# Idle products of 512 columns, and single chunk slots in the blocks from column 768 on

## The chip, the core and the metric

The kernel runs on one core of a Trainium2 chip. The core has five engines with queues of their own: TensorE (PE, matrix products; its weight loads are listed apart as PEld), VectorE (DVE), ScalarE (ACT), GpSimd (POOL) and SyncE (SP), which here issues nearly all DMA transfers. Products land in PSUM, of which the kernel's pools hold eight banks; DVE and ACT carry results from there to SBUF. The metric is the time of one execution on the device in microseconds, smaller being better.

## The reference

Two layers in a row. The first is a retention layer: for batch 8, 8 heads, 576 positions and head width 64,

```
scores = (q @ k.T) / sqrt(64)
D[i, j] = gamma_h ** (i - j)  if i >= j  else 0,   gamma_h = 1 - 2 ** (-5 - h)
x = (scores * D) @ v                    # laid out as 4608 tokens x 512
```

The second is a gated feed-forward layer on these 4608 tokens, with 1536 hidden columns:

```
out = (sigmoid(x @ w_gate) * (x @ w_val)) @ w_out     # 4608 x 512
```

Inputs and output are float32; products are made in bfloat16 with float32 sums.

## The kernel before

The decay is split into a factor on q and one on k (`qtab`, `ktab`), so that POOL and DVE, which cast q, k and v to bfloat16, multiply it in. The retention layer then runs in chunks of positions with a running state: the chunk's own part is `scores` (L476, tile row, PE line 483), a triangular `mask` on DVE (L495, tile pt) and `intra` (L504, tile val, PE line 509); what earlier chunks give is `inter` (L514, PE line 525), which multiplies q by the kept state; `products` (L486, PE line 491) makes the chunk's addition to the state, which `add_state` adds on DVE and `keep_state` casts (tile sb). The result is laid down transposed in `xT`, 512 by 4608, as the feed-forward layer wants it.

The first 768 columns of `xT` come from pairs of 128 positions, written out by hand (L816 to L998). The other columns come from 30 steps (`STEPS`), each with two pieces of 64 positions; step s fills the columns from 768 + 128 s on (the last two swapped). In the last piece of a batch (step 6 is the first of these) there is no `products`.

The feed-forward layer goes through `xT` in blocks of columns (`BLOCKS`, L1000): 256 columns at 512, 384 at 768 and at 1152, then 512 each. Within a block, `h_units` (L683) makes the gate and value products for 12 groups of hidden columns, and `op_units` (L746) the output products, 12 for each 128 tokens. Each of them yields after a unit: in the blocks of 384, 24 units of four h products, then 9 units of four op products. They use three PSUM banks (`ffn`) in turn. After the value product DVE multiplies by the sigmoid that ACT made (tile gv, L726).

Between these units, the loop from L1005 on places the chunk work, and this is what sets the order on all engines; there is no planner, the program's order is each queue's order. Two forms exist:

- `next_slot(s)` (L665, `slot` L529): one step. `intra` and `inter` of step s-1, then `scores`, `products` and `mask` of step s. The copies that empty the banks (`after`, L615) are put into `pending`, three parts, one for each later unit at which something may be placed. From step 6 on, the state casts of `after` go to POOL, before that to ACT.
- `next_two(vals, news)` (L675, `slot_of_two` L543): the values of up to two steps and the scores of two new ones in one group, with its copies in `after_two`. It uses two more banks for the second new step.

The values of a step stand in two PSUM banks (`VALS`), of which there is one each; the scores in two more (`ROWS`). In units of h of the larger blocks only every second unit takes something. In the block at 512 the loop places slots 0 to 3 (`SINGLE = 4`); every later block places two groups of two among its op units: ([3],[4,5]) and ([4,5],[6,7]) at 768, ([6,7],[8,9]) and ([8,9],[10,11]) at 1152, and so on, where the first list has the steps whose values are made and the second the new ones.

`casts_to(s)` (L654) issues, up to step s, the loads (SP), the casts (POOL), the DMA transpose of q and k (SP, tile T) and the cast of v. It is called ahead of the step that needs them, and at the start of each block from 768 on.

At the very start nothing can be computed until q and k are loaded. There `fill(n)` (L179) puts idle products on PE, of a zero tile into a spare bank that nobody reads; `fill` stands also between the first transposes and score products (L832 to L850). In all 24 units of n are issued.

## Time and profile before

| what | value |
|---|---|
| median of four runs | 329.26 us (329.12 to 330.04) |
| profiled execution | 329.12 us, of which the profile's span is 327.4 us |
| PE busy | 317.8 us, 97% of the span |
| DVE, ACT, POOL busy | 147.3, 139.6, 103.1 us |
| idle products (L182) | 96, 8.8 us busy, in the first 13 us |
| h products of the blocks (L698) | 426 and 426 recorded, 100.3 us busy each |
| op products (L765) | 353 recorded, 80.6 us busy |
| DMA moved | 55.16 MB, 168 GB/s in the mean |

A line of the timeline has the start and the length in us, the engine, the line of the kernel, the operation, what it writes and reads, the shape of the array used, the columns and the count; in brackets stands the idle time of the engine before it and what ended it. Products are pipelined: the length of one (219 ns for 128 columns, 379 ns for 512, at full speed) is longer than the step to the next, which is what counts in a stream. A few records of products are missing, which shows in the counts.

### The profile page before, as it was taken

How to read it: one execution, taken by the hardware profiler on the slowest of the kernel's cores; microseconds unless marked ns; L12 is line 12 of the kernel's file. 1: busy time of each engine (PE TensorE's matmuls, PEld its weight loads, DVE VectorE, ACT ScalarE, POOL GpSimd, SP SyncE). 2: the span in 40 equal slices, each digit the busy share in tenths (PEclk: the TensorE clock that was granted, in tenths of full speed). 3: DMA queues.
4: the chain of work that ended last, by engine and by line, in shares of the span. 5: the costliest groups of instructions: out<-in, count | busy, mean ns of one | idle time of the engine just before them, and what ended most of it. 6: DMA issues, size and time to landing. Idle time of an engine off the chain costs nothing.

```text
span 327.4 us, 8864 instructions
## 1 busy us (share of the span) xinstructions
PE 317.8 (97%) x3660; PEld 173.6 (53%) x3696; DVE 147.3 (45%) x331; ACT 139.6 (43%) x308; POOL 103.1 (31%) x136
## 2 busy tenths in 40 slices
PE   8899999999999999999999999999999999999995
PEld 8764457856655554455444544454445544544443
DVE  6845656654454463445334533444344433404410
ACT  6654545553344353324532553335334533343321
POOL 5674646453644093018200840074103000000000
PEclk9999999999999999999999999999999999999999
DMA  7999999999999689919791799169904910010003
GB/s 226 332 367 356 379 269 226 196 179 200 232 188 218 156 143 209 230 35 162 200 256 28 150 213 259 27 104 213 218 16 103 342 41 2 34 75 25 1 32 98
DMA packets 144794, 55.16 MB, mean 168 GB/s; under 512 B 125168, under 2 KB 136688, under 8 KB 144752
## 3 DMA queue, kind: packets, MB, share of 16 engines
q1 hardware_dynamic: 144608, 54.44, 69.9%
q8 instruction: 29, 0.48, 0.6%
q10 hardware_dynamic: 144, 0.13, 0.1%
q14 instruction: 13, 0.11, 0.1%
HBM read 37.75 MB, written 9.44 MB: 144 GB/s over the span
## 4 chain that ended last, share of the span: by engine, by line
PE 95%; ACT 1%; issue 1%; DVE 1%; ACTq 0%
PE h L698 50%; PE op L765 24%; PE op L952 3%; PE hv L802 3%; PE hg L802 3%; PE val L509 2%; PE idle L182 2%; PE row L483 1%; PE row L491 1%; PE val L525 1%; PE op L754 1%; PE qkp L329 1%; ACT qT L320 1%; PE hg L881 1%; PE hv L881 1%
## 5 line engine op out<-in xcount | busy, mean ns | idle before, releaser
L726 DVE TENSOR_TENSOR gv<-g,h 128x512 bf16<-128x512 bf16 (+1 forms) x96 | 62.8, 654 | 112.5 <-PE h L698 108.8
L698 PE MATMUL h<-xT,wg_sb 128*128 128x512 bf16 (+2 forms) x426 | 100.3, 355 | 0.3
L698 PE MATMUL h<-xT,wv_sb 128*128 128x512 bf16 (+2 forms) x426 | 100.3, 355 | 0.3
L722 ACT ACTIVATE g<-h 128x512 bf16<-128x512 f32 (+1 forms) x96 | 54.7, 570 | 93.6 <-PE h L698 83.1
L765 PE MATMUL op<-wo_sb,gv 128*128 128x512 bf16 x353 | 80.6, 379 | 2.5 <-issue 2.4
L698 PEld LDWEIGHTS <-wv_sb 128*128 128x128 bf16 x432 | 42.3, 98 | 40.7
L698 PEld LDWEIGHTS <-wg_sb 128*128 128x128 bf16 x432 | 42.0, 98 | 41.2
L765 PEld LDWEIGHTS <-gv 128*128 128x128 bf16 x372 | 35.2, 98 | 40.6
L288 POOL CAST v<-v 128x512 bf16<-128x512 f32 x29 | 17.7, 609 | 87.7 <-PE val L509 81.9
L283 POOL TENSOR_TENSOR qk<-k,ktab 128x512 bf16<-128x512 f32 x30 | 31.3, 1042 | 41.3 <-DMA k<-in_k_dram 28.6
L741 ACT COPY ob<-op 128x512 f32<-128x512 f32 x33 | 19.3, 585 | 32.9 <-PE op L765 30.0
L283 POOL TENSOR_TENSOR qk<-q,qtab 128x512 bf16<-128x512 f32 x28 | 29.2, 1042 | 2.5 <-DMA q<-in_q_dram 2.4
L567 ACT CAST xT<-val 128x256 bf16<-128x256 f32 x54 | 17.5, 381 | 26.7 <-PE val L525 19.8
L498 DVE TENSOR_TENSOR pt<-row,tri 128x256 bf16<-128x256 f32 x60 | 21.5, 418 | 2.4 <-PE row L491 1.5
L610 DVE TENSOR_TENSOR s<-s,row 128x256 f32<-128x256 f32 x39 | 16.3, 418 | 1.3
L459 ACT CAST sb<-s 128x256 bf16<-128x256 f32 x46 | 16.4, 421 | 0.2
L553 DVE COPY glance<-val 128x1 f32<-128x1 f32 x28 | 3.2, 154 | 26.5 <-PE val L525 23.6
L952 PE MATMUL op<-wo_sb,gv 128*128 128x512 bf16 x45 | 11.4, 379 | 0.3 <-issue 0.2
L525 PE MATMUL val<-T,sb 64*64 64x64 bf16 x368 | 10.0, 195 | 0.3 <-DVE glance L553 0.3
L509 PEld LDWEIGHTS <-v 64*64 64x64 bf16 x480 | 6.2, 108 | 7.1 <-issue 7.1
L809 DVE TENSOR_TENSOR gv<-g,hv 128x512 bf16<-128x512 bf16 x10 | 6.7, 684 | 7.0 <-PE hv L802 7.0
L182 PE MATMUL idle<-blank 128*128 128x128 bf16 x96 | 8.8, 262 | 1.1 <-DVE blank L170 1.1
(101 smaller groups left out, 235.1 us busy)
## 6 DMA issues: line engine op xcount, KB each, us to landing
out_dram<-ob SPq DMA_DIRECT2D x31, 256.0 KB, 3.6
k<-in_k_dram SPq DMA_DIRECT2D x26, 256.0 KB, 3.8
q<-in_q_dram SPq DMA_DIRECT2D x26, 256.0 KB, 4.0
v<-in_v_dram SPq DMA_DIRECT2D x26, 256.0 KB, 4.5
wg<-in_moe_w_gate_dram SPq DMA_DIRECT2D x12, 256.0 KB, 5.4
wv<-in_moe_w_val_dram SPq DMA_DIRECT2D x12, 256.0 KB, 5.1
wo<-in_moe_w_out_dram SPq DMA_DIRECT2D x12, 256.0 KB, 5.0
k32p<-in_k_dram SPq DMA_DIRECT2D x6, 256.0 KB, 5.0
```

Source lines behind the costliest of these rows:

```text
L283: eng.tensor_tensor(out=natural_qk[s][:, i].rearrange("p m (y d) -> p y m d", y=2), in0=by_halves(loaded[s][1 - i]), in1=tab, op=ALU.mult)
L288: eng(out=natural["v", s], in_=loaded[s][2])
L459: eng(out=state[key], in_=src)
L498: nc.vector.tensor_tensor(out=probs[s][:, y], in0=row_ps[s][y][:, 0], in1=tri.unsqueeze(1).to_broadcast([P, M, 64]), op=ALU.mult)
L567: nc.scalar.copy(out=xT[:, :, cols_of(s, i)], in_=val_ps[s][i])
L698: nc.tensor.matmul(out, lhsT=w_sb[:, kc, fc * P:(fc + 1) * P], rhs=xT[:, kc, t0 + a:t0 + e], start=(kc == 0), stop=(kc == NKC - 1))
L722: nc.scalar.activation(out=g[:, 0:n], in_=h1[:, 0:n], func=AF.Sigmoid)
L726: nc.vector.tensor_tensor(out=gvs[some[0]][:, a:e], in0=g[:, 0:n], in1=h2[:, 0:n], op=ALU.mult)
L741: (eng or on_act)(out=ob, in_=opp)
L765: nc.tensor.matmul(opp, lhsT=gvs[fc][:, nb * P:(nb + 1) * P], rhs=wo_sb[:, fc, :], start=(fc == 0), stop=(fc == NFC - 1))
L802: nc.tensor.matmul(ps, lhsT=(wg_sb if what == "g" else wv_sb)[:, kc, fc * P:(fc + 1) * P], rhs=xT[:, kc, 0:4 * P], start=(kc == 0), stop=( ...
L952: nc.tensor.matmul(opps[nb], lhsT=gvs[fc][:, nb * P:(nb + 1) * P], rhs=wo_sb[:, fc, :], start=(fc == 0), stop=(fc == NFC - 1))
```

## The change

It has two parts. First, a unit of `fill` is one product of 512 columns (the zero tile read four times over, into a whole bank), where it was four products of 128 columns. In all 24 products in place of 96.

Second, `SINGLE` becomes a list: the block at 512 places four single slots as before, the block at 768 three (4, 5, 6, at its h units 0, 10 and 20) and no group of two, the block at 1152 one (slot 7, at its h unit 0) and then the groups ([7],[8,9]) and ([8,9],[10,11]). From there on the groups are those of before. `casts_to` is no longer called at the start of a block; a group of two or a slot calls it alone. The spacing rule counts 5 units of 2048 from a block's end instead of 4, which leaves the slots of the block at 512 where they were.

```diff
     def idle_bank():
-        idle.append(ffn_psum.tile([P, P], FP32, tag="ffn", name=f"idle_{len(idle)}"))
+        idle.append(ffn_psum.tile([P, 4, P], FP32, tag="ffn", name=f"idle_{len(idle)}"))
...
     def fill(n):
 
-        for i in range(4 * n):
-            nc.tensor.matmul(idle[-1], lhsT=blank, rhs=blank, start=True, stop=True)
+        for i in range(n):
+            nc.tensor.matmul(idle[-1], lhsT=blank, rhs=blank.unsqueeze(1).to_broadcast([P, 4, P]), start=True, stop=True)
...
-    SINGLE = 4
+    SINGLE = [4, 3, 1]
...
-        end = slots + (SINGLE if w == 0 else 0)
+        end = slots + (SINGLE[w] if w < len(SINGLE) else 0)
...
-        if w == 0:
+        if w < 2:
             twos = []
-        else:
-            casts_to(slots + LEAD_CAST + 1)
...
-            elif slots < end and gone * (end - begin) >= (slots - begin) * (total - 4 * 2048):
+            elif slots < end and gone * (end - begin) >= (slots - begin) * (total - 5 * 2048):
                 next_slot(slots)
```

In the order of instructions on each engine, SP's queue is the same as before; POOL has two more instructions (the state casts of step 7, ahead of the casts of step 11), ACT ten more and DVE four more, since single slots copy their values in more and smaller pieces; PE has 72 products and 72 weight loads fewer, all idle ones.

## The prediction

> **What bounds the kernel now.** I read the shares of busy time first, then the chain of work that ended last, then TensorE's own timeline stretch by stretch. The first two say that TensorE (PE) is the limit nearly everywhere:

> ```profile
> PE 317.8 (97%) x3660; PEld 173.6 (53%) x3696; DVE 147.3 (45%) x331; ACT 139.6 (43%) x308; POOL 103.1 (31%) x136
> ...
> PE 95%; ACT 1%; issue 1%; DVE 1%; ACTq 0%
> ```

> So the price of an edit is what it does to PE's own queue, plus any wait that it makes PE meet. The change has two places: the idle products in the first 13 us, and the blocks from column 768 on. PE's timeline of the start (start, length, engine, line, tile, count):

> ```profile
> 1.05 4.45 PE L182 MATMUL idle<-blank 128*128 128x128 bf16 x40 [1.05 <-DVE blank L170]
> 5.29 0.63 PE L310 MATMUL kTp<-ident,kp 128*128 128x128 bf16 x4
> ...
> 6.14 1.03 PE L182 MATMUL idle<-blank 128*128 128x128 bf16 x12
> 7.25 0.42 PE L329 MATMUL qkp<-qT,kT 64*64 64x128 bf16 x16
> ...
> 7.83 0.61 PE L182 MATMUL idle<-blank 128*128 128x128 bf16 x8
> 8.28 0.39 PE L310 MATMUL qTp<-ident,qp 128*128 128x128 bf16 x4
> 8.50 0.83 PE L182 MATMUL idle<-blank 128*128 128x128 bf16 x12
> 9.49 0.42 PE L329 MATMUL qkp<-qT,kT 64*64 64x128 bf16 x16 [0.16 <-ACT qT L320]
> ...
> 12.36 0.83 PE L182 MATMUL idle<-blank 128*128 128x128 bf16 x12
> 13.12 0.41 PE L416 MATMUL pvp<-ptp,vp 64*64 64x128 bf16 x8
> ...
> 25.03 3.62 PE L802 MATMUL hg<-xT,wg_sb 128*128 128x512 bf16 x16
> ```

> The reader should see the step from one product to the next. The first 40 take 5.29 - 1.05 = 4.24 us, 106 ns each. The twelve from 8.50 last 0.83 us, of which the last one's own 0.219 us (the shortest of this group): 0.61/11 = 56 ns each. TensorE runs at half speed at first and at full speed from somewhere inside the twelve that begin at 6.14 (1.03 us is between the two rates). The last line gives products of 512 columns at full speed: 3.62 less 0.38 for the last, over 15, is 216 ns.

> The other place, from the same view further on:

> ```profile
> 58.24 0.60 PE L698 MATMUL h<-xT,wv_sb 128*128 128x256 bf16 x4
> 58.77 0.32 PE L509 MATMUL val<-pt,v 64*64 64x64 bf16 x16
> ...
> 59.43 0.61 PE L698 MATMUL h<-xT,wg_sb 128*128 128x256 bf16 x4
> ...
> 63.41 0.31 PE L509 MATMUL val<-pt,v 64*64 64x64 bf16 x14 [0.17 <-DVE xT L597]
> ...
> 71.75 0.81 PE L698 MATMUL h<-xT,wg_sb 128*128 128x384 bf16 x4
> 72.40 0.81 PE L698 MATMUL h<-xT,wv_sb 128*128 128x384 bf16 x4
> ```

> ```profile
> 93.77 0.32 PE L509 MATMUL val<-pt,v 64*64 64x64 bf16 x16
> ...
> 95.25 2.54 PE L765 MATMUL op<-wo_sb,gv 128*128 128x512 bf16 x11 [0.16 <-issue]
> 97.62 0.81 PE L698 MATMUL h<-xT,wg_sb 128*128 128x384 bf16 x4
> ...
> 123.69 1.03 PE L698 MATMUL h<-xT,wg_sb 128*128 128x512 bf16 x4
> ```

> Here the blocks begin at 71.75, 97.62 and 123.69, so they last 25.87 and 26.07 us. Their large products alone take 96 x 0.1625 (four in 0.65) + 36 x 0.216 = 23.38 us. What is left, 2.49 and 2.69 us, is two groups of chunk products each, and nothing else: PE never waits in these blocks. The "0.16 issue" before the line with x11 is a lost record (twelve were issued), not a wait.

> **The change, part by part.**

> *Idle products.* 72 products and 72 weight loads go; a unit of `fill` is one product of 512 columns, where it was four of 128. At half speed four steps are 0.427 us; a step of 512 at half speed is not in the trace, and twice its full-speed 0.216 is 0.432: no difference. At full speed a unit is 4 x 0.0558 = 0.223 against 0.216, 7 ns less. Most units hide something anyway: `fill(3)` at 6.14 and 8.50 and `fill(2)` at 10.30 end before ACT's qT or kT copy, which the next product waits for (9.49 line). On PE's path at full speed lie `fill(2)` at 7.83, `fill(1)` at 11.90, `fill(3)` at 12.36: six units, -0.04 us. The first `fill(10)` is also on the path: POOL's kp is ready at 3.77 + 1.04 = 4.81, and PE comes to it at 5.29; as long as before, it costs 0.

> [...]

> What the trace can't show is whether the other shape moves the moment of full speed. Bounds from rows: were it early enough for the first fill to end by 4.81, PE would gain 0.45 us there, but the next k tile is cast on POOL at 6.22 to 7.26 after its DMA, so the transposes at 7.59 could move to 7.30 at best: -0.3 us. Were it late, after 9.3, what PE does from 7.25 to 8.50 (1.25 us, all on the path) would take about twice as long: +1.2 less the 0.2 that waits for ACT, +1.0. The four runs of before spread over 0.92 us, which is about this. I take 0, since in either shape PE has no gap from 1.05 to 6.96.

> *Blocks.* Groups ([3],[4,5]) and ([4,5],[6,7]) of the block at 768, and ([6,7],[8,9]) of the next, become single slots 4, 5, 6 (units 0, 10, 20 of the block at 768), slot 7 (unit 0 of the next) and ([7],[8,9]). The products are the same 328. Price of before: the second group runs from 93.77, less 0.09 to enter, to 95.25 less the lost 0.216: 1.36. The first is 2.49 - 1.36 = 1.13. The group ([8,9],[10,11]) by the same reckoning (119.88 to 121.31) is 1.31, which leaves 1.38 for ([6,7],[8,9]). Sum 3.87.

> Price of after, from the single slots that stand before column 768. Slot 1, 64 products: PE could go on with h at 58.24 + 0.437 = 58.68 and does at 59.43: 0.75. Slot 0, 32 products: 52.95 + 0.437 to 53.86, 0.47. So about 9 ns a product and 0.19 for going in and out. Slots 4, 5 and 7 have 64 products, 0.75 each; slot 6, a last chunk without state products, 48: 0.61. Group ([7],[8,9]) has 88, eight fewer than ([3],[4,5]): 1.13 - 0.07 = 1.06. Sum 3.92, so +0.05. Bounds: the groups' internal delays vanish in ([7],[8,9]) (0.19 + 88 x 0.0088 = 0.96), -0.05; two groups more at 0.19 each and nothing else changed, +0.38. I take +0.05, by the row of a real slot.

> What is moved along with it. SP's queue keeps its order, DMA for DMA, so no load, transpose or store passes another. POOL gets two state casts of slot 7 ahead of the casts of chunk 11: they wait for DVE until about 101, and chunk 11, cast at 96.92 before, ends near 105; its transpose, at the longest landing (5.7 us) after an issue near 105, is there by 111, and PE wants it near 120. Chunk 4's transpose is issued from 64.26 and lands by 70.0; slot 4 wants it near 72.6. Chunks 5 and 6: issued at 71.42 and 76.98, wanted near 79.7 and 86.9. On ACT and DVE the copies of four slots now stand between sigmoids and gate products: in a pair of units (1.30 us of PE) ACT has 0.49 + 0.68 at most, DVE 0.56 + 0.28 + 0.41 = 1.25, and a bank of h is wanted again one pair later. The mask of a slot (0.75) falls into a pair that is itself 0.75 longer. All of it costs 0 while these margins hold.

> Sum: 329.12 (the profiled execution, span 327.4 and 1.7 around it) - 0.04 + 0.05 = 329.1. That execution is 0.14 below the median, so I expect a median of 329.2. About 0.2%, 0.66 us, is what a measurement of this kernel can tell from no change; 0.01 is far below it.

> **Rivals.**

> *Slots wait for a value bank (slower).* There is one bank each for the two halves of a chunk's values; slot s can't begin before the copies of slot s-1 have left them. Slot 2 shows the price: 62.49 + 0.437 = 62.93 to 64.06 is 1.13, 0.38 more than slot 1, and the releaser in the 63.41 line is DVE's leave_other. With four slots, +1.5: 330.7. Against it: slot 2 follows slot 1's last copy directly, where slot 4 has a unit of output products and one of h between (copies end at 70.96, slot at 72.4) and the others six units. It decides when DVE or ACT falls back by 1.4 us in slot 4, by 3.9 in the others.

> *Full speed comes later (slower).* Up to +1.0, 330.2; for it, only that the moment is not the program's to set; against it, PE is as full as before.

> *Full speed comes earlier (faster).* -0.3 at most by the DMA behind the second k tile: 328.9, still no change by the bound. To end on the faster side, the slots must also be cheaper than the groups by 0.4, or the idle stretches really shrink.

> *The moved groups buy nothing and cost the extra entries.* +0.38, 329.6: no change by the bound.

> **How the numbers follow.** Forecast as summed: 0.50. Early speed, 0.08, and the extra entries, 0.08, stay within 0.66 us too: 0.66 together. Slots that wait: 0.12. Late full speed in most runs: 0.08. Shorter idle stretches or cheaper slots, beyond 0.66: 0.14. So faster 0.14, same 0.66, slower 0.20. The range goes from 328.7 (early speed and the lower bound of the slots, with the spread of runs) to 330.2 (late speed, or two of four slots waiting).

> **What would show it.** Right: idle x10 from 1.05 to about 5.3 and a step of 216 ns later; h at 768 beginning near 71.7; slots near 72.5, 79.7, 86.9 and 98.1, each delaying h by 0.75; the blocks at 768 and 1152 lasting 23.38 + 2.11 = 25.5 and 23.38 + 0.75 + 1.06 + 1.31 = 26.5 us; no PE wait on DVE or ACT in them. Wrong: h at 768 beginning more than 0.5 us off 71.7 (the start moved), or a named wait ahead of val or h between 72 and 124 (the slots stall).

## The result and the profile after

The changed kernel takes 330.21 us in the median of 37 runs (329.13 to 333.22), the one before 329.25 us (59 runs, 328.64 to 330.36). The ratio is 1.0035, with a 95% interval of 1.0026 to 1.0045: slower by 0.35%, where I had forecast no change. (The ratio is not that of the two medians, which is 1.0029; it lies close to that of the means, so the long runs weigh in it.) The profiled execution took 329.93 us, its span 328.2 us, 0.8 us above that of before.

The runs of the changed kernel are of two kinds, told apart by the granted clock, the share of full speed that TensorE was given: of 38 with a record of the clock, 28 have a mean of 0.998 or more and a median of 329.87 us; ten have 0.993 to 0.995 and take 331.2 to 333.2 us. Of 74 runs of before that were made beside the experiments none has a clock below 0.998. So there are two amounts to explain: about 0.6 us in every run, and 2 us more in a quarter of them.

First the places that I had named. The page of the profile after, its busy times, two of its DMA queues and its chain:

```profile
span 328.2 us, 8732 instructions
...
PE 318.5 (97%) x3590; PEld 168.4 (51%) x3624; DVE 149.5 (46%) x335; ACT 139.1 (42%) x314; POOL 104.7 (32%) x138
...
q1 hardware_dynamic: 144608, 54.44, 69.6%
q8 instruction: 28, 0.46, 0.6%
...
PE 95%; issue 1%; ACT 1%; DVE 1%; ACTq 0%
```

TensorE is still the bound, with 0.7 us more of busy time. (ACT has 314 instructions where it had 308, six more and not ten.) The line to remember is that of queue 8, which moves instructions: 28 transfers, where the page of before has 29:

```profile
q8 instruction: 29, 0.48, 0.6%
```
The blocks, in TensorE's timeline after (start, length, engine, line, operation, tiles, array shape, columns, count):

```profile
72.47 0.81 PE L698 MATMUL h<-xT,wg_sb 128*128 128x384 bf16 x4
73.21 0.32 PE L509 MATMUL val<-pt,v 64*64 64x64 bf16 x16
...
73.89 0.82 PE L698 MATMUL h<-xT,wv_sb 128*128 128x384 bf16 x4
...
87.79 0.32 PE L509 MATMUL val<-pt,v 64*64 64x64 bf16 x16
...
98.03 0.81 PE L698 MATMUL h<-xT,wg_sb 128*128 128x384 bf16 x4
98.78 0.32 PE L509 MATMUL val<-pt,v 64*64 64x64 bf16 x16
...
99.46 0.82 PE L698 MATMUL h<-xT,wv_sb 128*128 128x384 bf16 x4
...
124.59 1.03 PE L698 MATMUL h<-xT,wg_sb 128*128 128x512 bf16 x4
```

The blocks last 98.03 - 72.47 = 25.56 and 124.59 - 98.03 = 26.56 us (forecast: 25.5 and 26.5). A slot of 64 products puts h off by 0.77 us (73.89 - 72.47 - 0.65), the shorter one at 87.79 by 0.60. No line of these blocks has a wait on DVE or ACT ahead of it. Together they take 52.12 us, where they took 51.94: +0.18.

The rest had happened before they began: h at 768 starts at 72.47, not 71.75, 0.72 us late. The start, in the same view:

```profile
1.05 4.45 PE L182 MATMUL idle<-blank 128*128 128x512 bf16 x10 [1.05 <-DVE blank L170]
5.29 0.63 PE L310 MATMUL kTp<-ident,kp 128*128 128x128 bf16 x4
...
7.23 0.42 PE L329 MATMUL qkp<-qT,kT 64*64 64x128 bf16 x16
...
15.13 0.44 PE L348 MATMUL st<-vp,kp 64*64 64x64 bf16 x16 [0.65 <-ACT sbd L358]
...
16.40 0.35 PE L348 MATMUL st<-vp,kp 64*64 64x64 bf16 x11
17.24 0.25 PE L348 MATMUL st<-vp,kp 64*64 64x64 bf16 x5 [0.49 <-issue]
17.43 0.40 PE L426 MATMUL pvp<-qT,sbd 128*128 128x128 bf16 x4
```

Up to the first score products everything is where it was (5.29 as before, 7.23 for 7.25). Then sixteen equal products, which write one tile and read two that were ready long ago, fall apart into eleven and five. The eleventh starts at 16.556, the twelfth at 17.240, where the step is 0.016 in the mean ((0.44 - 0.20)/15). "issue" says that the profile knows nothing that the engine waited for. In the timeline of before the same sixteen are one line:

```profile
16.22 0.44 PE L348 MATMUL st<-vp,kp 64*64 64x64 bf16 x16
16.59 0.40 PE L426 MATMUL pvp<-qT,sbd 128*128 128x128 bf16 x4
```

In the view of waits the second line here is the one entry of TensorE's in this stretch that before doesn't have (what waited, on what, us in total, times, longest):

```profile
PE st L348 <- ACT sbd L358: 0.7, 1, 0.7
PE st L348 <- issue: 0.5, 1, 0.5
```

This stop is nearly all of the 0.72 us: what follows it starts at 17.43 instead of 16.59, 0.84 late, of which 0.18 had come before it (at 12.3, where DVE's cast of q took 1.07 us instead of 0.79, beside POOL's cast of v), and 0.1 was won back later, at a place where before has a small gap of its own (1.15 us for eight products, 1.04 after):

```profile
19.28 1.15 PE L881 MATMUL hg<-xT,wg_sb 128*128 128x256 bf16 x8
```

```profile
20.11 1.04 PE L881 MATMUL hg<-xT,wg_sb 128*128 128x256 bf16 x8
```

What is missing at 16.56, by the records, is the code. The transfers of queue 8 are 16,384 bytes each (0.48 MB over 29, 0.46 over 28). TensorE's list of before has some 7,400 instructions, nearly all of them products and weight loads (3,696 loads and as many products), and 29 x 16,384 bytes over these is about 64 bytes each, so a transfer would hold 256 of them (an estimate from these counts); after, with 144 products and loads fewer, there is one transfer fewer. In the records of after the first of these transfers runs from 14.82 to 15.70, and the gap lies between the products that are instructions 448 and 450 of TensorE's list. In those of before the first transfer runs from 10.18 to 11.06, and TensorE comes to instruction 448 at 13.85, 2.8 us after the transfer's end. In after it comes there 0.86 us after the transfer's end and goes on 1.54 us after it. The small gap of before fits too: it is 0.12 us long, lies between instructions 704 and 706 (448 + 256), and TensorE goes on at 20.16, 1.38 us after the end of the second transfer (18.78).

That the transfer comes later against the border, by 2.8 - 0.86 = 1.9 us, is mostly a later start. TensorE passes instruction 192, one block ahead of the border, at 8.61 in before and at 11.77 in after. The transfer begins 1.57 and 3.05 us behind that; the way from 192 to 448 takes 5.24 and 4.79 us.

The theory that I then tested: the 72 idle products and 72 weight loads were padding between TensorE and the end of its code. Idle products of 512 columns use up the same time with a quarter of the instructions, so that the borders of the blocks of code come at other places of the work. In before and in after instruction 448 stands among small products, which use up two instructions every 16 ns; but in after TensorE comes there when the next block hasn't come. The rivals were that the new shape acts by the clock, or by its own length, or that the blocks make the difference.

### The profile page after: what moved, and what is told of

Its sections match the earlier page's. It is cut to its first block, busy times and chain, and to the rows that moved or that the text cites. A ratio compares the mean times of both kernels' runs of the same rounds, so it can differ in the third digit from the quotient of the medians.

```text
span 328.2 us, 8732 instructions
## 1 busy us (share of the span) xinstructions
PE 318.5 (97%) x3590; PEld 168.4 (51%) x3624; DVE 149.5 (46%) x335; ACT 139.1 (42%) x314; POOL 104.7 (32%) x138
## 4 chain that ended last, share of the span: by engine, by line
PE 95%; issue 1%; ACT 1%; DVE 1%; ACTq 0%
PE h L698 50%; PE op L765 24%; PE op L952 3%; PE hv L802 3%; PE hg L802 3%; PE val L509 2%; PE idle L182 2%; PE row L483 1%; PE row L491 1%; PE val L525 1%; PE op L754 1%; PE qkp L329 1%; ACT qT L320 1%; PE hv L881 1%; PE hg L881 1%
## 5 line engine op out<-in xcount | busy, mean ns | idle before, releaser
L698 PE MATMUL h<-xT,wv_sb 128*128 128x512 bf16 (+2 forms) x426 | 100.3, 355 | 0.3
L698 PE MATMUL h<-xT,wg_sb 128*128 128x512 bf16 (+2 forms) x426 | 100.3, 355 | 0.3
L765 PE MATMUL op<-wo_sb,gv 128*128 128x512 bf16 x355 | 80.7, 379 | 2.2 <-issue 2.1
L698 PEld LDWEIGHTS <-wg_sb 128*128 128x128 bf16 x432 | 42.0, 98 | 41.2
L698 PEld LDWEIGHTS <-wv_sb 128*128 128x128 bf16 x432 | 42.0, 98 | 40.4
L765 PEld LDWEIGHTS <-gv 128*128 128x128 bf16 x372 | 35.3, 98 | 40.9
L567 ACT CAST xT<-val 128x256 bf16<-128x256 f32 x46 | 15.0, 381 | 22.6 <-PE val L525 19.5
L509 PEld LDWEIGHTS <-v 64*64 64x64 bf16 x480 | 6.2, 108 | 7.5 <-issue 7.5
L182 PE MATMUL idle<-blank 128*128 128x512 bf16 x24 | 8.7, 493 | 1.1 <-DVE blank L170 1.1
```

The source lines that it names most:

```text
L698: nc.tensor.matmul(out, lhsT=w_sb[:, kc, fc * P:(fc + 1) * P], rhs=xT[:, kc, t0 + a:t0 + e], start=(kc == 0), stop=(kc == NKC - 1))
L765: nc.tensor.matmul(opp, lhsT=gvs[fc][:, nb * P:(nb + 1) * P], rhs=wo_sb[:, fc, :], start=(fc == 0), stop=(fc == NFC - 1))
```

## The experiments

### The two halves by themselves

`fill` of 512 columns with the blocks of before:

```diff
 (the kernel before)
-        for i in range(4 * n):
-            nc.tensor.matmul(idle[-1], lhsT=blank, rhs=blank, start=True, stop=True)
+        for i in range(n):
+            nc.tensor.matmul(idle[-1], lhsT=blank, rhs=blank.unsqueeze(1).to_broadcast([P, 4, P]), start=True, stop=True)
```

> The idle products of 512 columns alone; the blocks are those of before. Code theory: PE's instructions arrive in blocks of 256 (16,384 bytes a time on the instruction queue), and 144 fewer idle instructions move a block's border from the idle stretch into the small products near 16.5 us. It expects a gap of about 0.7 us between two equal st products near 16.5 us, with nothing that they wait for, a first instruction transfer near 14.8 us in place of 10.2 us, about +0.5 to +0.7 us on the usual run, and some runs 2 us longer still. Rival 1, the blocks made the loss: no change here, ratio 1.000. Rival 2, the shape of the idle products changes when TensorE's full speed comes: a change of the step from 427 to 216 ns away from about 6.6 us, and no gap near 16.5 us.

And the single slots with idle products of 128 columns:

```diff
 (the kernel before)
-    SINGLE = 4
+    SINGLE = [4, 3, 1]
...
-        if w == 0:
+        if w < 2:
             twos = []
-        else:
-            casts_to(slots + LEAD_CAST + 1)
```

> Only the single slots in the blocks at 768 and 1152; the idle products are the 96 of 128 columns of before, so the borders of the instruction blocks in the first 13 us are those of before. Code theory: no gap near 16.5 us, the blocks at 768 and 1152 together 0.1 to 0.2 us longer (52.1 against 51.9 us), ratio 1.0003 to 1.0006, no runs 2 us longer. Rival 1, the blocks made the loss: ratio 1.002 to 1.0035, with the long runs among them. Rival 2 (shape): as the code theory.

Measured: the idle products alone 329.85 us (12 runs), ratio 1.0037 (1.0009 to 1.0066); the blocks alone 329.23 us (11 runs), ratio 1.0001 (0.9990 to 1.0013). The loss belongs to the idle products. With these alone the seven runs of a clock of 0.998 or more have a median of 329.5 us, 0.3 above before, where 0.5 to 0.7 was expected. The profile of the blocks alone, taken at a granted clock of 0.85, keeps the sixteen st products in one line:

```profile
16.35 0.42 PE L348 MATMUL st<-vp,kp 64*64 64x64 bf16 x16
```

The timeline with the idle products alone has the gap at the same two instructions, twice as long, and what comes after it takes longer too:

```profile
16.76 0.35 PE L348 MATMUL st<-vp,kp 64*64 64x64 bf16 x11
18.31 0.32 PE L348 MATMUL st<-vp,kp 64*64 64x64 bf16 x5 [1.20 <-issue]
...
19.67 1.04 PE L881 MATMUL hg<-xT,wg_sb 128*128 128x256 bf16 x4
```

Four products of 256 columns take 1.04 us here, 0.61 before. The profiled execution, 333.79 us, is one of five of the twelve with a low mean clock, and the stretches of one microsecond show where (us, then length, TensorE's busy share and count, granted clock, DMA share, GB/s):

```profile
15.00:16.00 1.00, 0.51 (x19) 1.00 1.08 363
16.00:17.00 1.00, 0.98 (x39) 1.00 1.00 340
17.00:18.00 1.00, 0.11 (x8) 0.92 1.08 373
18.00:19.00 1.00, 0.69 (x9) 0.50 1.11 403
```

The clock falls to one half at 17.85 us and comes back at 24.67. That is the second amount: in this execution 6.8 us at half speed right behind the gap.

### Moving the border, and nothing else

If the code is late because of where its border lies, putting the border back must remove the gap from after, and moving it must bring the gap into before. Five of the first ten idle units are replaced by small idle products of 64 x 64, which take many instructions and about the same time (in the run 2.22 us for 77 of them, from 1.05 to 3.27, where five of the ten units take 2.12, half of 4.24):

```diff
 (the kernel after; the second kernel is the one before, with small(76))
+    def small(n):
+
+        for i in range(n):
+            p0 = 64 * (i % 2)
+            nc.tensor.matmul(idle[-1][p0:p0 + 64, 0, 0:64], lhsT=blank[0:64, 0:64], rhs=blank[0:64, 0:64],
+                             start=True, stop=True)
+
-    fill(10)
+    small(77)
+    fill(5)
```

In the kernel after, 77 of them (144 instructions more in all) put the borders where before has them. In the kernel before, 76 make 256 instructions more than after has, so that a border lies where after has it, one block further on.

> The changed kernel, with five of the ten first idle units replaced by 77 products of 64 columns with 64-column weights (about the same 2.1 us, if two go side by side), so that PE has as many instructions ahead of the real work as before, and the instruction borders lie where they lay before. The other 19 idle units keep 512 columns. Code theory: no gap near 16.5 us, first instruction transfer near 10 us, no runs 2 us longer, ratio 1.000 to 1.001. Rival 2 (shape): the loss stays, ratio about 1.003. Rival 1 (blocks): the loss stays.

> The kernel of before, idle products of 128 columns and blocks as they were, with five of the first ten idle units replaced by 76 such small products: PE has 112 instructions more ahead of the real work, which is 256 more than the changed kernel has, so the instruction borders lie where the changed kernel has them. Code theory: a gap of 0.5 to 0.7 us near 16.5 us, ratio 1.0015 to 1.0035, some runs 2 us longer. Rivals 1 and 2: no change, ratio 1.000, since shape and blocks are those of before.

Measured: after with the borders of before 329.83 us (11 runs), ratio 1.0018 (1.0008 to 1.0028); before with the borders of after 332.03 us (6 runs), ratio 1.0085 (1.0053 to 1.0117). The profile of the first has no gap: its st products stand in one line of sixteen again. In the second the sixteen fall apart where they do in after, between instructions 704 and 706 (448 + 256), at 17.388 and 17.698, with the transfer at 15.43 to 16.36. That is 0.31 us in the profiled execution, and the timeline keeps the sixteen in one line, of 0.72 us:

```profile
17.23 0.72 PE L356 MATMUL st<-vp,kp 64*64 64x64 bf16 x16
```

Four of the six runs of the second have a clock of 0.990 to 0.995, none of the eleven of the first. So the gap follows the border of the code, with 512 columns or with 128. But both are slower than I had expected, above the ranges of 1.000 to 1.001 and of 1.0015 to 1.0035. For the second, four low clocks in six runs are more than I had reckoned with. For the first, its start shows a reason:

```profile
1.05 2.28 PE L188 MATMUL idle<-blank 64*64 64x64 bf16 x77 [1.05 <-DVE blank L170]
...
6.56 1.49 PE L182 MATMUL idle<-blank 128*128 128x512 bf16 x3
7.98 0.49 PE L337 MATMUL qkp<-qT,kT 64*64 64x128 bf16 x16
```

`fill(3)` runs at half speed here (1.49 us, 1.04 in after), and the first score products start at 7.98 instead of 7.23. The clock's record goes to full at 8.16 us in this execution and at 7.92 in the other; in after it was 6.59. By these two profiles the padding was not neutral: with small products ahead full speed came later.

### Padding with the products of before

The first ten units as they were, four products of 128 columns, in the kernel after: 60 instructions more, no small products. And two of the ten only, 12 instructions more, which move the gap by six products and don't remove it:

```diff
 (the kernel after; the second kernel has fill_by_four(2) and fill(8))
-    fill(10)
+    def fill_by_four(n):
+
+        for i in range(4 * n):
+            nc.tensor.matmul(idle[-1][:, 0], lhsT=blank, rhs=blank, start=True, stop=True)
+
+    fill_by_four(10)
```

> The changed kernel with its first ten idle units made of four products of 128 columns again (40 products); the other 14 units and the blocks stay changed. PE has 60 instructions more ahead of the real work than in the changed kernel, so its instruction borders come 60 instructions earlier in the work and the request for the next block falls ahead of the waits at 9.5 and 11.5 us instead of behind them. Code theory: first instruction transfer at 9 to 12 us, no gap near 16.5 us, no long runs, ratio 1.000 to 1.0008. Rival (shape of the idle products, or the blocks): ratio stays near 1.0035, long runs stay.

> As the changed kernel, but two of its first ten idle units are four products of 128 columns: 12 instructions more, no time more. Code theory: the border moves by six products and their weight loads, and the gap with it: in the changed kernel the 16 st products near 16.5 us are split 11 and 5, here they should be split 5 and 11. The request for the block still comes late, so the loss and the long runs stay, ratio 1.002 to 1.004. If the gap had to do with what st or the engines around it do, it would stay behind the 11th product.

Measured: ten units by four 329.44 us (12 runs), ratio 1.0013 (1.0004 to 1.0021), a little above the 1.0008 expected, no gap, no run with a low clock; the transfer ran from 11.56 to 12.98, 2.9 us before TensorE came to instruction 448. Two units by four 330.23 us (11 runs), ratio 1.0034 (1.0020 to 1.0048), two runs with a clock of 0.995; its profile splits the sixteen into five and eleven, as forecast by the border alone:

```profile
16.47 0.25 PE L354 MATMUL st<-vp,kp 64*64 64x64 bf16 x5
17.51 0.35 PE L354 MATMUL st<-vp,kp 64*64 64x64 bf16 x11 [0.79 <-issue]
```

Ten units by four is the kernel after with most of its loss gone, by an edit that adds 30 idle products.

### What the rest of it is

The 0.13% that remains could be the new blocks or the fourteen other units of 512 columns. This kernel has the same idle products as the last one of ten units by four, and the blocks of before:

```diff
 (ten units by four, fourteen of 512 columns; the other lines of the blocks as before too)
-    SINGLE = [4, 3, 1]
+    SINGLE = 4
```

> Before, with the first ten idle units left as four products of 128 columns, the other fourteen as one of 512, and the blocks of before. With those first ten and the new blocks the ratio was 1.0013 [1.0004, 1.0021], with no gap in the small products; this run tells which half that remainder belongs to. Theory 1, the new blocks cost what their stretches showed in the profile (52.12 us against 51.94, +0.18 us) or more: here nothing is left, 329.25 us, ratio 0.9997 to 1.0005. Theory 2, the fourteen units of 512 columns cost it (the stretch from the first transpose to the first score products): ratio 1.001 to 1.0015 again. No gap in the st products in either, and no run with a mean clock of 0.995 or less.

Measured: 329.06 us (11 runs) beside 329.07 for before, ratio 1.0003 (0.9994 to 1.0011), no gap, clock 0.999 or more in all runs. So the shape of 512 columns by itself, in these fourteen units, costs nothing that can be measured, once the code is in time. With the new blocks there are two runs without a gap: the blocks alone, 1.0001 (0.9990 to 1.0013), and ten units by four, 1.0013 (1.0004 to 1.0021). What the profile shows of the blocks, +0.18 us or 0.0005, lies inside both intervals, and nothing finer can be told from these runs.

### Does the gap take the clock with it, or the late code?

Two attempts. First, another wait of TensorE's, the 0.65 us ahead of the st products at 15.13, is filled with three idle products, so that the gap stands alone:

```diff
 (the kernel after)
     pair_intra(0, 1, 1)
+    fill(3)
     pair_st(0, 1)
```

> The changed kernel with a fill(3) (three idle products of 512 columns, 0.65 us) put where PE waits 0.65 us for ACT's sbd copy, near 14.3 us. Six instructions more ahead of the st products: by the code theory the gap stays and splits them 8 and 8. Theory of the long runs: PE drops to half speed when it was idle too long in a stretch of some 3.4 us, of which the gap and this wait are parts; with the wait filled the long runs (10 of 38 of the changed kernel) should become fewer or vanish, the usual runs staying at +0.5 to +0.7 us: ratio 1.001 to 1.0025. If the drop hangs on the gap alone, as many long runs as before, ratio 1.003 to 1.005.

Measured: 330.36 us (7 runs), ratio 1.0039 (1.0025 to 1.0052), one of the seven with a low clock (0.993). The gap moved as forecast, to eight and eight, but grew to 1.13 us:

```profile
14.24 0.82 PE L182 MATMUL idle<-blank 128*128 128x512 bf16 x3
15.00 0.44 PE L348 MATMUL st<-vp,kp 64*64 64x64 bf16 x16
...
16.27 0.31 PE L348 MATMUL st<-vp,kp 64*64 64x64 bf16 x8
17.52 0.31 PE L348 MATMUL st<-vp,kp 64*64 64x64 bf16 x8 [0.93 <-issue]
```

One in seven against ten in 38 tells nothing, and the usual runs were slower than expected by what the gap had grown.

Second, the stop without the late code. In the kernel before, TensorE is made to wait at 16.22 for two ScalarE copies, or for four:

```diff
 (the kernel before; range(4) in the second kernel)
+    late = consts.tile([P, 256], BF16)
...
     pair_intra(1, 1, 0)
+    for i in range(2):
+        nc.scalar.copy(out=late, in_=blank.unsqueeze(1).to_broadcast([P, 2, P]))
+    nc.tensor.matmul(idle[-1], lhsT=blank, rhs=late[:, 0:P], start=True, stop=True)
     pair_st(1, 0)
```

> Before, with two ScalarE copies (0.37 us each) and one idle product that waits for them put ahead of the st products at 16.22 us. No code arrives late here; TensorE just waits at the place where the kernel after waits for its code, for about 0.75 us (ScalarE is done with its state casts at 16.17, the copies end near 16.95). Theory 1, a stop of TensorE at this place is enough to lose the clock in some executions: usual runs near 330.0 us (ratio about 1.002), and one to four of about twelve 2 us longer, with a mean granted clock of 0.995 or less. Theory 2, the loss belongs to the late code: all runs near 330.0, none at 331.2 or more, clock 0.998 or more in all.

> As the run with two copies, with four: TensorE waits about 1.5 us at 16.22 us, as long as the longest gap seen with late code (1.39 us). Theory 1, the stop is enough: usual runs near 330.75 us (ratio about 1.0046), and a larger part of them, four to eight of about twelve, 2 to 3 us longer than that, with a mean clock of 0.995 or less. Theory 2: all near 330.75 with the clock at 0.998 or more.

Measured: with two copies 330.16 us (11 runs), ratio 1.0037 (1.0024 to 1.0051); eight runs at 329.5 to 330.3, and three at 331.0 to 331.3 with a clock of 0.993 to 0.995. With four copies 332.49 us (6 runs), ratio 1.0107 (1.0086 to 1.0127); all six have a clock of 0.990 to 0.995, more than I had expected of it. The timeline with four copies, and its stretches of one microsecond:

```profile
16.08 0.63 PE L417 MATMUL pvp<-ptp,vp 64*64 64x128 bf16 x24
18.28 0.22 PE L870 MATMUL idle<-late,blank 128*128 128x128 bf16 x1 [1.57 <-ACT late L869]
```

```profile
15.00:16.00 1.00, 0.71 (x20) 1.00 0.93 319
16.00:17.00 1.00, 0.69 (x25) 1.00 0.90 298
17.00:18.00 1.00, 0.00 (x0) 1.00 0.99 343
18.00:19.00 1.00, 0.72 (x19) 0.80 1.06 374
19.00:20.00 1.00, 1.00 (x12) 0.50 1.05 399
```

Here the wait has a name (with two copies the same line has 0.70 in place of 1.57), no code is late, and the clock goes to one half all the same. A stop of TensorE at this place is enough. With two copies, a stop of the same size as in after, the kernel behaves like after in both amounts: the usual runs up by 0.9 us, three of eleven longer by a further 1.2 or so.

All runs together (low: mean clock 0.995 or less):

| kernels | runs | low |
|---|---|---|
| late code at the st products (after; idle products alone; before with shifted borders; two units by four; other wait filled) | 74 | 22 |
| a stop of 0.7 us there, code in time | 11 | 3 |
| a stop of 1.6 us there, code in time | 6 | 6 |
| neither (before; blocks alone, without its profiled execution, which had a clock of 0.85; after with borders back; ten units by four, with both kinds of blocks) | 118 | 0 |

## Why the clock falls in some runs only

This part is read from the records of the profiled executions, not tested by a run. The stretches of the clock's record between its first change and the end have lengths of 3.413 us times a whole number: 13.653 us at full and 6.827 at half in the run of the idle products alone, 13.653 and 3.413 in the run with four copies, 320.853 (94 x 3.413) in before and after. The first change came at 4.19, 4.94, 5.75, 5.95, 6.33, 6.55, 6.55, 6.59 and 7.00 us in the nine executions in which only large products stand at the start, so it has no fixed place in the kernel: after, the idle products alone and the other wait filled begin with the same ten units, and have it at 6.59, 4.19 and 6.33. What decides the clock no record shows. The reading below, by cells of 3.413 us, is an estimate from these lengths.

If one cuts TensorE's timeline into such cells, with the clock's first change as their origin, and adds up the time within each cell in which no product runs (after the clock is up, to 37 us), these cells have the most:

| execution | cell, us | time idle in it | clock after it |
|---|---|---|---|
| before | 13.38 to 16.79 | 0.67 | full |
| after | 13.42 to 16.83 | 0.75 | full |
| two units by four | 15.99 to 19.40 | 0.79 | full |
| before with shifted borders | 14.75 to 18.16 | 0.79 | full |
| other wait filled | 16.56 to 19.98 | 0.93 | full |
| idle products alone | 4.19 to 7.61 | 0.93 | full |
| four copies | 4.94 to 8.36 | 0.99 | full |
| idle products alone | 14.43 to 17.85 | 1.41 | half |
| four copies | 15.18 to 18.60 | 1.70 | half |

In after's profiled execution the border of two cells (16.83) cut the gap in two: 0.65 us of the earlier wait and 0.1 of the gap fell into one cell, 0.41 of the gap into the next. With the first change at another time the whole gap and the earlier wait would fall into one cell, 1.15 us or more. If idle time that meets in one cell is what takes the clock, that would give what the runs show, a fixed program with two kinds of runs, and none in kernels in which no more than 0.7 us of idle time can meet in one cell there. In these rows the clock stayed at full after 0.99 us and less and went to half after 1.41 and 1.70; none lies between, so they don't tell whether 1.15 us is enough. The size fits: a mean clock of 0.995 over 328 us is 0.005 x 328 / 0.5 = 3.3 us at half speed, about one cell, which costs half of that, 1.6 us, where the low runs of after are 1.9 us longer in the median.

Two kernels don't fit by their profiles alone. Where the other wait is filled, no more than 0.93 us can meet in one cell, and one run of seven is low; in before with shifted borders no more than 0.79 us, and four of six are low. The gap has another length in each profile, 0.31 to 1.39 us, and a longer one in those runs would explain it; no record shows it.

The two executions that lost the clock did so with TensorE at work for 2.0 and 1.7 us of the cell before.

The same cells laid over the start: in the run with 77 small products the cell from 1.34 to 4.75 us was full of products, 1.93 us of it the small ones, and the clock rose one cell later, at 8.16; in the run with 76 the same at 7.92. In all nine others the first cell without idle time, or with 0.27 us at most, was followed by full speed.

## Why the prediction was wrong

**The bound and the blocks: right.** TensorE stayed the bound. The blocks were to cost +0.05 us, with bounds of -0.05 and +0.38; they cost +0.18 in the profile, and 1.0001 (0.9990 to 1.0013) by themselves. The forecast slots of 0.75 measured 0.77, 0.79 and 0.77, the shorter one 0.60 for 0.61, ([7],[8,9]) 1.09 for 1.06. The starts of the slots lay where forecast, but for the 0.72 us by which all was late. Everything priced at nothing because it was "moved along" on SP, POOL, ACT and DVE did cost nothing: no wait on any of these stands in the blocks.

**The idle products as durations: right.** The first ten end at the same 5.29, the step of 512 columns is the 216 ns that I took from another row, and the fourteen units behind them by themselves cost nothing (1.0003, 0.9994 to 1.0011, with the code in time). That the idle stretches would really shrink, for which part of the 0.14 of the faster side stood, no run shows: the first ten units last the same 4.24 us in the profiles of before and after, and fill(3) at full speed (at 8.50 and 8.53) 0.83 and 0.81.

**The failed step: "72 products and 72 weight loads go; a unit of fill is one product of 512 columns, where it was four of 128", priced at -0.04 us.** I went on from it at once to durations, and so took an instruction for nothing but its time on the array. It also takes up room in TensorE's code, about 64 bytes by the estimate above. With 144 instructions fewer ahead of the work, TensorE passed instruction 192 at 11.77 instead of 8.61. The block of code from instruction 449 on came too late for the st products near 16.5, and TensorE stood still for 0.67 us there. In place of -0.04 us the idle products cost 0.3 to 0.6 us in the usual runs, and 2 us more in part of the runs. I had gone through the queues that the change moves work past, SP's and POOL's, and left out the one that serves TensorE itself, though the page shows it ("q8 instruction", 29 transfers) and the records say when each comes. With these at hand the gap could have been suspected, though not its length: in before TensorE had come to about the 255th instruction when the first transfer began, in after to the 339th, and why they differ I can't say.

**The rivals.** None was it. "Full speed comes later" had the nearest time (330.2), but by another mechanism: in the profiled execution after, full speed came at 6.59 us, in before at 6.55, and over the other profiles at 4.19 and 6.33 where the first ten units are of 512 columns, at 4.94 to 7.00 where they are of 128. What it had right is that the clock matters for this edit; I looked for it at 5 us and not behind the gap at 17. "Slots wait for a value bank" (+1.5) is excluded by the run of the blocks alone and by the blocks of the profile, which have no such wait. Of the +0.38 of "the moved groups buy nothing" the profile shows 0.18.

**The range** ended at 330.2, at a bound that came from a different cause, and the median of 330.21 lies beside it. Without the ten long runs the median would be 329.87, inside the range and 0.62 us above before, just within the 0.66 that I had called no change.

The signs that I had named for being wrong did work: "h at 768 begins more than 0.5 us off 71.7 (the start moved)" is what happened.

What stays open: what sets the delay of a transfer of code. In all twelve profiles the first began after TensorE had passed instruction 192, when it had come to instruction 197 to 376; the delay was 0.25 to 1.6 us in the six that passed 192 before 9 us, and 1.8 to 3.8 in the six that passed it later. With the 1.57 us of before, the transfer would have been in time in after as well (an estimate: 11.77 + 1.57 + 0.88 for the transfer + 1.54 = 15.76, before 16.56). So also open is why the gap is 0.3 us in one execution and 1.4 in another, and whether the low clock of the long runs of after always falls behind this gap, since only the profiled executions have a record of when.

## What to carry to other kernels

An edit that changes the number of TensorE's instructions moves the borders of its code (here 12 instructions more moved the gap by six products, and six instructions by three): look up the instruction queue's transfers in the trace, find which products stand at the new border and how long before them the transfer ends, and mistrust a dense run of small products there. An idle time of TensorE can cost more than its length: here 0.7 us of stop came with 2 us more in a quarter of the runs, so one profile tells little and the granted clock of every run has to be read. By the two profiles with small ones (full speed at 7.92 and 8.16 us, against 4.19 to 7.00), idle products that are to bring the clock up were best large on the array (128 x 128); 128 or 512 columns, in fourteen units, made no difference here (1.0003, 0.9994 to 1.0011) with the code in time.
